# Attention and gated FFN on one Trainium2 core: the last addition of VectorE's exponential moved to accumulating DMAs, more quads on VectorE, and the second chunk of queries in two

## The chip, the core and the metric

The kernel runs on one core of one Trainium2 chip. A core has five engines with a queue each, and each works through its queue in order: TensorE (PE; its weight loads are shown as PEld), VectorE (DVE), ScalarE (ACT), GpSimd (POOL) and SyncE (SP). SP starts all the DMAs of the kernel before. The metric is the device time in microseconds (us), as the median of several runs. A profile describes one single execution.

## The reference

One transformer block of 2048 tokens, width 640, 32 heads of 20 elements, with a gated FFN of width 1728. Arrays are bf16.

```python
x = A_x                                        # [1, 2048, 640]
h = x + _A_ref(_layernorm(x), A_wqkv, A_wo)    # softmax attention, 32 heads of 20, then @ wo
h2 = h + _B_ref(_layernorm(h), B_w_gate, B_w_up, B_w_down)   # (gelu(x Wg) * (x Wu)) Wd
return h2
```

The scores are 32 x 2048 x 2048 = 134 million numbers, and the exponential of every one of them has to be computed. That is the bulk of the element-wise work.

## The kernel before

**Tiles and quads.** Scores are computed transposed: keys lie on the 128 partitions and queries along the row. A *tile* is one PSUM bank of 512 columns of scores for one head. A *quad* is the four tiles of four heads that share a group g of the heads. There are 2048 tiles, or 512 quads. Queries are taken in *chunks* (`SIZES`: 512, 512, 256, 256, 256, 128, 128). A chunk is divided into *slots* of 16 quads (64 tiles) each; there are 32 slots, numbered 0 to 31. With 512 queries a slot is one head group, with 256 queries it is two groups, with 128 it is four.

**Two engines compute the exponential.** Most tiles go to ACT: one ACTIVATE reads two or three neighbouring PSUM banks (1024 or 1536 columns) and writes bf16 to `pts` or `pts2`. Some quads go to DVE instead; `D_QUADS` gives their number for each slot, 68 in all. DVE's way (`d_exp`, L881 and the lines after it) reads a tile from PSUM, scales it and writes int16 (this is the eviction, 512 columns at a time). When two tiles (1024 columns; slots below 18) or four tiles (2048 columns, "wide"; slots from 18 on) are together in a buffer `v`, six more operations follow: mask out the low bits to `df`; a linear function to `dw`; `dw*dw`; `dw` times the masked bits; `v += dw`; and a closing scale, whose int16 result, read as bf16, is the exponential. All six run on DVE. The buffers for `v` are taken in turn from pools named e (first chunk), l (slots 8 to 17) and w (from slot 18 on); they lie in spare parts of SBUF and in the parts of `qt_all` whose queries are done. There is one `df` and one `dw` for each pool.

**PSUM.** Eight banks. ACT's tiles alternate between two sets of banks (`PAT`): sets of three and two (five banks), or, in the slots named in `SIX` (8 to 15), three and three. Bank 6 collects the sums of probabilities and V for a slot. The banks that are left, 7 and 5 or in the six-bank slots 7 alone, hold everything else (projections, FFN, transposes). A DVE tile takes one of these, or in a six-bank slot the third bank of a set.

**Units.** A *unit* is what one ACTIVATE covers: two or three tiles, with at most one DVE tile beside it. `D_LEAD` says by how many tiles a slot's DVE tiles are computed ahead of their place (24 for later slots). `D_LAG` (9) says how many units after the last DVE tile of a quad PE's products with V for this quad are put in the program.

**What sets the order.** A planner (`Sched`) orders everything. Each operation has an engine, a planned duration, a priority, and what it reads and writes; the planner plays the program through with these durations and so fixes each engine's order. In it the engines then wait for each other by semaphores. A DMA has a planned issue time on its engine and a planned latency until it lands (`lat`). PE gets filler products (`sc.pad`, `sc.warm`) where it would be idle too long.

**The rest of a slot and a chunk.** At the end of a slot, `epilogue` copies bank 6 to `osb` (two buffers, used in turn), PE transposes it (L1039), and DVE divides by the sums of probabilities into `o_nat`, which has four places of 128 queries. When a chunk's last slot is done, `post` runs its second half as background work: DMA transposes (in the tail and for the first chunk PE's) of `o_nat`, the output projection and the residual into `h_sb` (L1087), LayerNorm with its rsqrt on POOL, the normalised rows into `xn_t`, DMA transposes of these to `hnT`, then the gate products, whose raw results wait in `ha_f` (L1155), one batch of gelu on ACT with a table load before and after it, the up products and their multiplication (L1169), the down products and the last residual (L1204), and the store to `out`. `BASE` says which of the four places of `h_sb`, `hnT` and `o_nat` a chunk begins at, so a chunk's `post` has to wait for an earlier chunk that used the same places. `MERGE` names chunks whose gelu waits for that of the next chunk; it is empty.

Of the kernel before, what the change touches and what calls it, by code (L numbers as in the profile page):

```python
# [7 lines left out]
ALU = mybir.AluOpType  # L8
AX = mybir.AxisListType
FP32 = mybir.dt.float32  # L10
# [305 lines left out]
SIZES = (512, 512, 256, 256, 256, 128, 128)  # L316
BASE = (0, 0, 0, 2, 0, 2, 3)
SIX = tuple(range(8, 16))
# [26 lines left out]
def bass_sequential_preLN__mha_block__glu_gated_geglu__prompt_kernel(  # L345
# [12 lines left out]
    with ExitStack() as es:  # L358
# [3 lines left out]
        def sb(name, shape, dt=BF16):  # L362
            return es.enter_context(nc.sbuf_tensor(name, shape, dt))
# [17 lines left out]
        sel = sb("sel", [128, NA, H])  # L381
        zer = sb("zer", [128, 32])
        sel0 = sb("sel0", [128, 4, 32])
# [46 lines left out]
        aq = [carve(512) for _ in range(2)] + [sq[:], xn_t[:, 0, 0:512], xn_t[:, 1, 0:512]]  # L430
# [26 lines left out]
        dw1 = carve(1024).bitcast(F16)  # L457
        carve = carver(qt_all[:, 0, :, :].rearrange("p g s -> p (g s)"), NG * 512)
        dvw += [carve(2048).bitcast(I16) for _ in range(2)]
        dv.append(dvx[:].bitcast(I16))  # L460
        zb = dvx[:].rearrange("p (i s) -> p i s", i=2)
        dv0 = [ha_f[:, 1024 * i:1024 * i + 1024].bitcast(I16) for i in range(5)]
        df0, dw0 = ha_f[:, 5120:6144], ha_f[:, 6144:7168].bitcast(F16)
        carve = carver(qt_all[:, 1, :, :].rearrange("p g s -> p (g s)"), NG * 512)
        df2 = carve(2048)
        dw2 = carve(2048).bitcast(F16)
# [42 lines left out]
        cst(I("memset", sel[:], -1.0), "sel", 160)  # L509
        cst(I("affine_select", out=sel[:], in_=sel[:], compare_op=ALU.is_ge, fill=0.0, base=0,  # L510
              pattern=[[128, NA], [-DH, H]], channel_multiplier=1), "sel", 160)
        cst(I("affine_select", out=sel[:], in_=sel[:], compare_op=ALU.is_ge, fill=0.0, base=DH - 1,
              pattern=[[-128, NA], [DH, H]], channel_multiplier=-1), "sel", 160)
        cst(I("memset", sel0[:], 0.0), "sel0")
# [77 lines left out]
        def ln_apply(eng, src, dst, dkey, t, rkeys, prio, first=False):  # L592
            if eng == "act":
                fn = I("activation", dst, src, ACT.Identity, bias=nm[:, t:t + 1], scale=rs[:, t:t + 1])
            else:
                fn = I("tensor_scalar", dst, src, mu[:, t:t + 1], rs[:, t:t + 1], ALU.add if first else ALU.subtract,
                       ALU.mult)
            return op(eng, fn, 0.82 if eng == "act" else c_dve(D, 0.46), prio,
                      reads=list(rkeys) + [("mu", t), ("rs", t)] + ([("nm", t)] if eng == "act" else []), writes=[dkey])
# [68 lines left out]
        def aqk(t):  # L668
            return ("xn", t - 3) if t >= 3 else ("aq", t)
# [99 lines left out]
        def q_bound0(banks, prio):  # L769
# [3 lines left out]
                bank(bk), sel0[:].rearrange("p j e -> p (j e)"), aq[0], start=True, stop=True),  # L773
# [77 lines left out]
        d_cur = [None]  # L851
        d_late = []
# [9 lines left out]
        def d_exp(b, tile, prio, u):  # L862
# [15 lines left out]
            keys = [("dv", i)] + ([("dv", ("l", k)) for k in ((0, 1), (2, 3), ())[i[1]]] if kind == "w" and i[1] < 3 else [])  # L878
            aft = tuple(e_ops) + (q_done(0) if c else ()) + (q_done(1) + tuple(d_late) if kind == "w" else ()) + \
                (q_done(2) if kind == "w" and i[1] > 2 else ())  # L880
# [12 lines left out]
            d(I("tensor_scalar", dw, zi, CA / OCT, CB, ALU.mult, ALU.add), 0.265, ["df"], ["dw"])  # L893
# [130 lines left out]
        def epilogue(s_, bk, d_sums):  # L1024
# [4 lines left out]
            op("dve", I("tensor_copy", osb[:, s, :], PS[:, 512 * 6:512 * 7]), c_dve(512), P_QK,  # L1029
               reads=[("O", s_)], writes=[("osb", s)], rel=[bk], after=tuple(d_sums))  # L1030
# [7 lines left out]
            for tt in range(4):  # L1038
                op("pe", lambda eng, tt=tt: eng.transpose(bank(b2)[:, tt * 128:(tt + 1) * 128],  # L1039
                                                          osb[:, s, tt * 128:(tt + 1) * 128], identf[:]),  # L1040
                   c_mm(128, 2.5), P_EPI, mode="full", reads=[("osb", s), "identf"], writes=[key], acq=[b2] if tt == 0 else [],
                   after=tuple(aft) if tt == 0 else ())
# [22 lines left out]
        def post(c, first_banks, banks, tail):  # L1065
# [33 lines left out]
            for tt in range(tb, tb + nt):  # L1099
                t = q0 // 128 + tt - tb  # L1100
                ln_apply("dve", h_sb[:, tt, :], xn_t[:, t % 2, :], ("xn", t % 2), t, [("h", tt, 0), ("h", tt, 1)], pd)
                if tail:
                    transposes(xn_t[:, t % 2, :], [("xn", t % 2)], hnT[:, :, tt * 128:(tt + 1) * 128], ("hnT", tt),
                               first_banks, p, "act", after=first)
                else:
                    dma_transposes(xn_t[:, t % 2, :], [("xn", t % 2)], hnT[:, :, tt * 128:(tt + 1) * 128], ("hnT", tt),
# [189 lines left out]
```

## Time and profile before

| | |
|---|---|
| median of 3 runs | 914.34 us (914.05 to 917.4) |
| the profiled execution | 916.19 us |
| its span, first to last instruction | 914.2 us |
| granted TensorE clock, mean | 0.998 |
| ACT busy | 881.1 us (96% of the span) |
| PE busy | 824.1 us (90%) |
| DVE busy | 794.1 us (87%) |
| POOL busy | 48.2 us (5%) |
| DMA queue of SP | 32.89 MB, 12.9% of 16 engines' time |

The profile gives one line to each group of equal instructions: line, engine, operation, what is written and read, count, then busy time and mean length of one. Many operations are recorded by one helper (line 366), so such groups are told apart by their tiles and shapes. A PSUM bank is called `ps`. Tables of stages give, for each stretch of time, the busy time and number of instructions of each engine. Consecutive instructions on one engine overlap at their edges, so a mean length is longer than the time for which one holds the engine. PE's ends are modelled, so a busy PE is not PE at its peak.

### The profile page before, as it was taken

The numbers are of one execution on the slowest core, as the hardware profiler recorded it, in microseconds if no ns is written. First come the engines' busy times: TensorE is split into PE (matmuls) and PEld (weight loads), VectorE is DVE, ScalarE is ACT, GpSimd is POOL, SyncE is SP. The second block draws the span as 40 slices with busy tenths as digits, with TensorE's granted clock in tenths as the row PEclk, the third lists the DMA queues.
The fourth block names the chain that finished last, engine by engine and source line by source line (L and its number), as shares of the span: only waits on it lengthen the run. The fifth ranks groups of instructions, "written<-read, shape, count | busy, mean of one in ns | idle before, by whom it ended". The sixth has DMA issues, their size and how long they took to land.

```text
span 914.2 us, 22759 instructions
## 1 busy us (share of the span) xinstructions
PE 824.1 (90%) x9952; PEld 351.2 (38%) x10017; DVE 794.1 (87%) x1458; ACT 881.1 (96%) x789; POOL 48.2 (5%) x149
## 2 busy tenths in 40 slices
PE   3999999999898878899798989999999989998998
PEld 1432322222232222233233333344454445556666
DVE  8869998999899986987899997999998998779753
ACT  7999999999999999999999999999999999999982
POOL 5000000000011000000021000002010000010000
PEclk9999999999999999999999999999999999999999
DMA  7211020323801000000122000000100000110000
GB/s 259 83 31 33 23 62 25 90 67 76 291 25 30 1 1 1 1 8 16 37 35 27 1 1 1 16 30 10 37 16 18 29 1 3 36 27 10 10 17 15
DMA packets 39514, 34.33 MB, mean 38 GB/s; under 512 B 19436, under 2 KB 36936, under 8 KB 39416
## 3 DMA queue, kind: packets, MB, share of 16 engines
q1 hardware_dynamic: 39416, 32.89, 12.9%
q8 instruction: 78, 1.28, 0.6%
q14 instruction: 20, 0.16, 0.1%
HBM read 20.12 MB, written 8.09 MB: 31 GB/s over the span
## 4 chain that ended last, share of the span: by engine, by line
ACT 57%; PE 23%; DVE 17%; POOL 1%; issue 1%; DMA 0%; DVEq 0%
ACT pts L366 36%; ACT rege L366 19%; PE ps L947 6%; DVE qt_all L366 5%; PE ps L366 4%; PE ps L1120 4%; PE ps L663 4%; PE ps L1200 3%; DVE rege L366 3%; DVE qt_all L881 2%; DVE rege L881 2%; DVE rege L1169 1%; DVE rege L1155 1%; ACT L366 1%; DVE regw L701 1%
## 5 line engine op out<-in xcount | busy, mean ns | idle before, releaser
L366 ACT ACTIVATE pts<-ps 128x1024 bf16<-128x1024 f32 (+1 forms) x470 | 561.6, 1349 | 3.6 <-PE ps L947 1.5
L947 PE MATMUL ps<-qt_all,kt_all 32*128 32x256 bf16 (+2 forms) x3584 | 309.2, 289 | 44.8 <-ACT pts L366 22.0
L366 ACT ACTIVATE rege<-ps 128x1024 bf16<-128x1024 f32 (+1 forms) x233 | 288.9, 1342 | 1.9 <-PE ps L366 1.3
L947 PEld LDWEIGHTS ps<-qt_all,kt_all 32*128 32x128 bf16 x3584 | 101.4, 92 | 265.1 <-ACT pts L366 135.6
L366 DVE TENSOR_TENSOR qt_all<-qt_all 128x2048 f16<-128x2048 f16 (+3 forms) x186 | 175.0, 941 | 2.6
L1120 PE MATMUL ps<-rege,regw 128*128 128x256 bf16 (+2 forms) x952 | 151.0, 288 | 12.1 <-ACT rege L366 3.5
L366 PE MATMUL ps<-pts,v_all 128*21 128x256 bf16 (+2 forms) x2070 | 125.4, 291 | 0.4 <-DVE osb L366 0.4
L881 DVE TENSOR_SCALAR qt_all<-ps 128x512 int16<-128x512 f32 x128 | 87.4, 683 | 20.0 <-PE ps L947 19.5
L1120 PEld LDWEIGHTS ps<-rege,regw 128*128 128x128 bf16 x980 | 72.5, 98 | 71.2 <-issue 30.5
L881 DVE TENSOR_SCALAR rege<-ps 128x512 int16<-128x512 f32 x128 | 87.5, 684 | 11.0 <-PE ps L947 10.3
L366 PE MATMUL ps<-rege,v_all 128*21 128x256 bf16 (+2 forms) x1214 | 91.9, 294 | 2.6 <-DVE rege L366 2.3
L663 PE MATMUL ps<-regw 128*128 128x320 bf16 (+1 forms) x340 | 82.5, 353 | 4.2 <-ACT regw L611 1.7
L366 DVE TENSOR_SCALAR qt_all<-qt_all 128x1024 f16<-128x1024 int16 (+2 forms) x153 | 84.0, 557 | 1.9
L1200 PE MATMUL ps<-regw,rege 128*128 128x320 bf16 x448 | 80.6, 302 | 2.0 <-DVE rege L1169 1.0
L366 DVE TENSOR_TENSOR rege<-rege 128x1024 f16<-128x1024 f16 (+1 forms) x90 | 61.4, 683 | 0.8
L366 PEld LDWEIGHTS ps<-pts,v_all 128*21 128x21 bf16 x2070 | 45.1, 91 | 34.8 <-issue 29.3
L1169 DVE TENSOR_TENSOR rege<-rege,ps 128x512 bf16<-128x512 bf16 (+1 forms) x53 | 35.6, 677 | 21.9 <-PE ps L1120 21.8
L1200 PEld LDWEIGHTS ps<-regw,rege 128*128 128x128 bf16 x448 | 36.3, 97 | 34.4 <-issue 16.0
L366 DVE TENSOR_SCALAR rege<-rege 128x1024 int16<-128x1024 int16 (+2 forms) x115 | 48.3, 436 | 0.5
L366 PE MATMUL ps<-kt_all,zer 128*32 128x512 bf16 x560 | 46.9, 384 | 0.0
L663 PEld LDWEIGHTS ps<-regw 128*128 128x128 bf16 x360 | 28.4, 99 | 45.0 <-issue 24.5
L366 PEld LDWEIGHTS ps<-rege,v_all 128*21 128x21 bf16 x1214 | 31.1, 91 | 22.6 <-issue 12.1
(105 smaller groups left out, 587.9 us busy)
## 6 DMA issues: line engine op xcount, KB each, us to landing
rege<-in_A_x_dram SPq DMA_DIRECT2D x6, 640.0 KB, 5.2
q_rows<-regw SPq DMA_DIRECT2D x20, 128.0 KB, 1.7
out_dram<-rege SPq DMA_DIRECT2D x16, 160.0 KB, 2.5
regw<-in_B_w_gate_dram SPq DMA_DIRECT2D x1, 2160.0 KB, 8.4
regw<-in_B_w_up_dram SPq DMA_DIRECT2D x1, 2160.0 KB, 13.4
regw<-in_B_w_down_dram SPq DMA_DIRECT2D x1, 2080.0 KB, 19.8
kt_all<-k_rows SPq DMA_DIRECT2D x12, 160.0 KB
qt_all<-q_rows SPq DMA_DIRECT2D x12, 160.0 KB
```

What stands on the lines that cost most here:

```text
L366: return lambda eng: getattr(eng, method)(*args, **kwargs)
L663: yield op("pe", lambda eng, l=l, r=r, k=k: eng.matmul(bank(bk, n), l, r, start=(k == 0), stop=(k == len(steps) - 1)), c_mm(n) + cold, pri ...
L701: e = op("dve", lambda eng: eng.tensor_copy(dst, bank(bk)), c_dve(512), prio, reads=[key], writes=[dkey], rel=[bk], after=after)
L881: d_ops.append(op("dve", lambda eng: eng.tensor_scalar(v[:, 512 * h:512 * h + 512], bank(b), EXP_MUL, -32000.0, ALU.mult, ALU.max), c_dve( ...
L947: return lambda eng: eng.matmul(out()[:, kk * nq:(kk + 1) * nq], kt_all[32 * j:32 * j + 32, g, kt * 128:(kt + 1) * 128], qt_all[32 * j:32 ...
L1120: op("pe", lambda eng, a=a, f=f, fi=fi: eng.matmul(bank(bk)[:, fi * nq:(fi + 1) * nq], w[:, a, F0[f]:F0[f] + 128], hnT[:, a, 128 * tb:128 ...
L1155: cp.append(op("dve", lambda eng, bg=bg, fv=fv, w=w: eng.tensor_copy(fv, bank(bg, w)), c_dve(w), p, reads=[kg], writes=hkeys(k), rel=[bg], ...
L1169: hdone.append(op("dve", lambda eng, bu=bu, fv=fv, w=w: eng.tensor_tensor(fv, fv, bank(bu, w), ALU.mult), c_dve(w), p, reads=[ku] + hkeys( ...
L1200: op("pe", lambda eng, f=f, o=o, hf=hf, bk=bk: eng.matmul(bank(bk, 320), ha_f[:, o:o + 128], wd[:, f, hf * 320:(hf + 1) * 320], start=(f = ...
```

## The change

- The last addition of DVE's exponential, `v += dw`, becomes a DMA that POOL issues and that accumulates from SBUF into SBUF, in slots 1, 2, 3, 5 and 9 to 31 (`DA_SLOTS`). The product before it is written as int16 for that. The planner counts 0.95 us for the issue and then 4.67 us (1024 columns) or 7.0 us (2048 columns) until the sum has landed. DVE's closing scale waits for it. Slots 0, 4, 6, 7 and 8 keep the addition on DVE. There are 90 such DMAs.
- `dw` gets two buffers for each pool, and the pools of `v` get more: six, six, and four (six once the third quarter of the queries is done).
- `D_QUADS`: slots 18 to 27 have three DVE quads each instead of three and two in turn; 73 quads in all.
- `D_LEAD` for slots from 11 on is 42 tiles instead of 24; `D_LAG` is 8 instead of 9.
- The second chunk of 512 queries becomes two chunks of 256, and `MERGE` joins the gelu, up and down steps of these two, so that they run together after slot 15. The six-bank slots are 8 to 11 alone.
- For room in SBUF: `osb` has one buffer; `xn_t` and `sq` are gone, and LayerNorm's rows are written over `o_nat`; `sel`, `sel0` and some of the buffers of the first phase lie in the new buffers `dvx` and `dwx`.

```diff
-SIZES = (512, 512, 256, 256, 256, 128, 128)
-BASE = (0, 0, 0, 2, 0, 2, 3)
-SIX = tuple(range(8, 16))
+SIZES = (512, 256, 256, 256, 256, 256, 128, 128)
+BASE = (0, 0, 2, 0, 2, 0, 2, 3)
+SIX = tuple(range(8, 12))
...
-D_LAG = 9
-MERGE = ()
+D_LAG = 8
+MERGE = (1,)
+DA_ISSUE, DA_LAT = 0.95, 7.0
+DA_SLOTS = (1, 2, 3, 5) + tuple(range(9, 32))
...
-D_QUADS = (1,) + (2,) * 15 + (2, 2) + (3, 2) * 5 + (2, 2, 2, 2)
+D_QUADS = (1,) + (2,) * 15 + (2, 2) + (3,) * 10 + (2, 2, 2, 2)
...
-D_LEAD = ((0,) * 8, (0, 10, 20) + (24,) * 21)
+D_LEAD = ((0,) * 8, (0, 10, 20) + (42,) * 21)
...
-        osb = sb("osb", [128, 2, 512], FP32)
+        osb = sb("osb", [128, 512], FP32)
...
-        sq = sb("sq", [128, 512])
-        xn_t = sb("xn_t", [128, 2, D])
-        dvx = sb("dvx", [128, 1024])
+        dvx = sb("dvx", [128, 2048])
+        dwx = sb("dwx", [128, 2048])
...
-                pool = [(kind, i) for i in range(5 if kind != "w" or CHUNKS[slots[units[u][0][0]][0]][0] >= 1536 else 3)]
+                busy |= set(("w", k) for k, ks in enumerate(((0, 1), (2, 3), (), (4, 5))) if any(("l", x) in busy for x in ks))
+                n_ = {"e": 6, "l": 6, "w": 6 if CHUNKS[slots[units[u][0][0]][0]][0] >= 1536 else 4}[kind]
+                pool = [(kind, i) for i in range(n_)]
...
+            d_alt[0] += 1
+            a_ = d_alt[0] % len(dw)
+            dk = ("dw", a_)
+            dw = dw[a_]
+            di, dw = dw.bitcast(I16), dw.bitcast(F16)
...
-            d(I("tensor_tensor", dw, dw, dw, ALU.mult), 0.53, ["dw"], ["dw"])
-            d(I("tensor_tensor", dw, dw, zi, ALU.mult), 0.53, ["df", "dw"], ["dw"])
-            d(I("tensor_tensor", v, v, dw, ALU.add), 0.53, ["dw", ("dv", i)], [("dv", i)])
+            d(I("tensor_tensor", dw, dw, dw, ALU.mult), 0.53, [dk], [dk])
+            if tile[0] in DA_SLOTS:
+                d(I("tensor_tensor", di, dw, zi, ALU.mult), 0.53, ["df", dk], [dk])
+                d_ops.append(op(POOL, I("dma_start", v, di, accum_op=ALU.add), DA_ISSUE, prio, reads=[dk], writes=[("dv", i)],
+                                sem="da%s%d" % i, lat=DA_LAT * (w_ + 1) / 3))
+            else:
+                d(I("tensor_tensor", dw, dw, zi, ALU.mult), 0.53, ["df", dk], [dk])
+                d(I("tensor_tensor", v, v, dw, ALU.add), 0.53, [dk, ("dv", i)], [("dv", i)])
...
-                ln_apply("dve", h_sb[:, tt, :], xn_t[:, t % 2, :], ("xn", t % 2), t, [("h", tt, 0), ("h", tt, 1)], pd)
+                ln_apply("dve", h_sb[:, tt, :], o_nat[:, tt, :], [("on", g, tt) for g in range(NG)], t, [("h", tt, 0), ("h", tt, 1)], pd)
```

More of the change, by code (lines that the diff above doesn't have):

```diff
@@ L429, in bass_sequential_preLN__mha_block__glu_gated_geglu__prompt_kernel @@
         qoff = carve(512)
-        aq = [carve(512) for _ in range(2)] + [sq[:], xn_t[:, 0, 0:512], xn_t[:, 1, 0:512]]
+        aq = [carve(512) for _ in range(2)] + [dvx[:, 1024:1536], dvx[:, 1536:2048], dwx[:, 0:512]]
         carve = carver(regw, W_WORDS)
@@ L668, in aqk @@
         def aqk(t):
-            return ("xn", t - 3) if t >= 3 else ("aq", t)
+            return ("aq", t)
         STEP = {1: (1, 3), 2: (3, 4), 3: (4, 6), 4: (6, 8)}
@@ L772, in q_bound0 @@
             w_readers.append(op("pe", lambda eng: eng.matmul(
-                bank(bk), sel0[:].rearrange("p j e -> p (j e)"), aq[0], start=True, stop=True),
+                bank(bk), sel0.rearrange("p j e -> p (j e)"), aq[0], start=True, stop=True),
                 c_mm(512), prio, mode="full", util=0.213, reads=[("aq", 0), "sel0"], writes=[key], acq=[bk]))
@@ L851, in bass_sequential_preLN__mha_block__glu_gated_geglu__prompt_kernel @@
         d_cur = [None]
+        d_alt = [0]
         d_late = []
@@ L1028, in epilogue @@
             nt = nq // 128
-            op("dve", I("tensor_copy", osb[:, s, :], PS[:, 512 * 6:512 * 7]), c_dve(512), P_QK,
-               reads=[("O", s_)], writes=[("osb", s)], rel=[bk], after=tuple(d_sums))
+            op("dve", I("tensor_copy", osb[:], PS[:, 512 * 6:512 * 7]), c_dve(512), P_QK,
+               reads=[("O", s_)], writes=["osb"], rel=[bk], after=tuple(d_sums))
             b2 = Bank(*BGC[c])
```

42 lines of the change are left out of this document (23 added, 19 removed).

## The prediction

> **What bounds the kernel now.** I read four views: the page's first and fourth parts, a table of busy time by stage, the groups by shape, and the timeline of single stretches. First, the whole:
>
> ```profile
> PE 824.1 (90%) x9952; PEld 351.2 (38%) x10017; DVE 794.1 (87%) x1458; ACT 881.1 (96%) x789; POOL 48.2 (5%) x149
> ...
> ACT 57%; PE 23%; DVE 17%; POOL 1%; issue 1%; DMA 0%; DVEq 0%
> ...
> q1 hardware_dynamic: 39416, 32.89, 12.9%
> ```
>
> ScalarE (ACT) is the busiest engine and holds most of the chain that ended last; DMA is nearly idle. Now by stage, with cuts at the ends of slots 7, 11, 15, 17 and 27 and at the last exponential (columns: length, then busy us and count of PE, PEld, DVE, ACT, POOL, then clock, DMA share, GB/s):
>
> ```profile
> 33.30:242.60 209.30, 194.68 (x1560) 60.01 (x1580) 186.52 (x374) 207.03 (x182) 0.62 (x1) 1.00 0.23 67
> 242.60:352.40 109.80, 94.02 (x802) 28.32 (x811) 98.55 (x197) 109.74 (x93) 8.04 (x28) 1.00 0.14 43
> 352.40:453.90 101.50, 89.01 (x772) 28.94 (x779) 86.39 (x164) 101.50 (x88) 0.00 (x0) 1.00 0.05 14
> 453.90:506.10 52.20, 46.19 (x640) 19.02 (x647) 48.43 (x98) 52.05 (x47) 8.43 (x28) 1.00 0.18 27
> 506.10:773.20 267.10, 252.14 (x3337) 116.02 (x3349) 250.78 (x379) 265.84 (x231) 10.91 (x28) 1.00 0.06 14
> 773.20:881.60 108.40, 101.42 (x2333) 65.07 (x2336) 82.28 (x137) 106.49 (x92) 7.28 (x28) 0.98 0.10 20
> 881.60:914.20 32.60, 27.99 (x381) 22.98 (x379) 13.18 (x32) 11.02 (x14) 0.00 (x0) 1.00 0.05 16
> ```
>
> From 33.3 to 881.6 us ACT is busy 843 of 848 us, so what the change is worth there is ACT time taken away, as long as VectorE (DVE) keeps up. DVE's room differs: 11% idle in slots 0-7, 10 to 15% in slots 8-15, but 6% in slots 18-27 (250.78 of 267.10). There, slot by slot:
>
> ```profile
> 506.10:531.60 25.50, 23.86 (x303) 9.62 (x306) 25.27 (x38) 25.30 (x24) 0.00 (x0) 1.00 0.01 1
> ...
> 564.50:590.20 25.70, 23.63 (x325) 9.67 (x327) 25.51 (x38) 25.70 (x24) 0.00 (x0) 1.00 0.07 15
> 590.20:612.70 22.50, 22.10 (x301) 9.84 (x300) 20.52 (x31) 22.41 (x21) 0.00 (x0) 1.00 0.10 31
> ```
>
> Slots with three DVE quads (18, 20) leave DVE under 0.3 us; one with two (21) leaves 2 us. All five added quads go into slots of this stage, so DVE is the second bound.
>
> **The change, part by part.**
>
> *Five more quads on DVE (68 to 73).* A quad is four tiles of 512 columns, so ACT loses 20 tiles. Its shapes:
>
> ```profile
> L366 ACT ACTIVATE pts<-ps 128x1536 bf16<-128x1536 f32 x249 | 377.3, 1550 | 3.4 <-PE ps L947 1.5 <-PE ps L366 0.9
> L366 ACT ACTIVATE pts<-ps 128x1024 bf16<-128x1024 f32 x221 | 243.9, 1122 | 0.2
> L366 ACT ACTIVATE rege<-ps 128x1536 bf16<-128x1536 f32 x121 | 185.4, 1551 | 1.9 <-PE ps L366 1.3 <-PE ps L947 0.4
> L366 ACT ACTIVATE rege<-ps 128x1024 bf16<-128x1024 f32 x112 | 124.2, 1116 | 0.0
> ...
> 328.27 3.11 ACT L366 ACTIVATE pts<-ps 128x1536 bf16<-128x1536 f32 x2
> 330.95 3.12 ACT L366 ACTIVATE rege<-ps 128x1536 bf16<-128x1536 f32 x2
> ```
>
> A tile is 1550 - 1122 = 428 ns. The last two rows start 2.68 us apart, so instructions overlap and a three-tile one holds the engine for 1.34 us: 1.34 - 3 x 0.428 = 0.056 us is fixed. 20 tiles: -8.56 us. Walking the loop that forms units with the old constants gives 370 and 333 instructions of three and two tiles, as the rows have (249+121, 221+112); with the new ones 356 and 344 (1756 tiles, which is (512-73) x 4). Three fewer: -0.17 us. That already includes four more in slots 12-15, where the six-bank pattern becomes three and two banks. ACT: -8.7 us.
>
> *The final addition of DVE's exp goes to an accumulating DMA on POOL*, except in slots 0, 4, 6, 7 and 8. What DVE pays:
>
> ```profile
> L366 DVE TENSOR_TENSOR rege<-rege 128x1024 int16<-128x1024 int16 x30 | 20.5, 682 | 0.2
> ...
> L366 DVE TENSOR_TENSOR qt_all<-qt_all 128x2048 f16<-128x2048 f16 x51 | 61.9, 1214 | 0.6
> L881 DVE TENSOR_SCALAR qt_all<-ps 128x512 int16<-128x512 f32 x69 | 47.0, 683 | 5.3 <-PE ps L947 5.1
> L366 DVE TENSOR_SCALAR qt_all<-qt_all 128x2048 int16<-128x2048 int16 x36 | 24.1, 677 | 0.2
> L366 DVE TENSOR_TENSOR qt_all<-qt_all 128x2048 int16<-128x2048 int16 x18 | 21.8, 1209 | 0.1
> L1155 DVE CAST rege<-ps 128x512 bf16<-128x512 f32 x24 | 16.3, 680 | 0.0
> ```
>
> A wide quad (slots 18 on) is 4 evictions of 0.68, 3 multiply-or-mask operations of 0.68 and 3 two-input operations of 1.21: 8.4 us; without the last addition 7.2. In slots 18-27: 25 additions go (-30 us), 5 quads come (+36 us): +6 us, on a stage that ACT wants 8.7 us shorter (258.4). DVE would stand at 256.8 of it. Elsewhere it gains: 8 early quads and 18 in slots 9-17 lose two additions of 0.68 each (-35 us), slots 28-31 lose 8 of 1.21 (-10 us); all beside ACT, so worth nothing by itself.
>
> *The second chunk of queries in two, its two FFNs joined.* Table loads stay: six batches of gelu before and after, over the same columns. But the first half's output projection, LayerNorm and gate products can start after slot 11 instead of slot 15. They wait for the first chunk's last outputs, since they reuse its rows of h_sb:
>
> ```profile
> 402.95 22.61 SPq L366 DMA_DIRECT2D out_dram<-rege  x3
> 437.06 0.39 SPq L366 DMA_DIRECT2D rege<-in_A_x_dram  x1
> 437.50 0.51 SPq L366 DMA_DIRECT2D out_dram<-rege  x1
> 457.04 6.02 SPq L366 DMA_TRANSPOSE rege<-o_nat  x4
> ...
> 437.50:453.90 16.40, 12.10 (x128) 3.60 (x130) 13.81 (x27) 16.40 (x16) 0.00 (x0) 1.00 0.17 51
> ```
>
> So they fall into about 415-455 us, where DVE and PE have room, and 7 gate evictions and the like (7 x 0.68 + 4 x 0.48 and LayerNorm: about 8 us of DVE) leave the time after slot 15. I count 6 of them off the tight stage: DVE 251 of 258.4 us, 97%. 256-wide products instead of 512-wide double PE's weight loads for these queries; the row of slots 16-17, 256 wide already, has ACT at 52.05 of 52.20, so I cost it at nothing; PE's idle time of 12% in slots 12-15 is the cover, and without it the extra loads (512 of scores at 92 ns by the next row, four at a time) would be some 12 us.
>
> ```profile
> L947 PEld LDWEIGHTS ps<-qt_all,kt_all 32*128 32x128 bf16 x3584 | 101.4, 92 | 265.1 <-ACT pts L366 135.6 <-ACT rege L366 70.0 <-issue 31.6
> ```
>
> *The DMA itself.* DVE runs in order, and its closing scale waits for the landing; evictions of scores are queued behind it, PE's next scores wait for those banks, and ACT for PE. The order gives issue and landing 0.95 + 4.67 = 5.6 us for 1024 columns (256 KB), 0.95 + 7.0 = 7.95 us for 2048 (512 KB). No accumulating DMA is in the trace. Nearest rows (KB each, us to landing):
>
> ```profile
> rege<-in_A_x_dram SPq DMA_DIRECT2D x6, 640.0 KB, 5.2
> q_rows<-regw SPq DMA_DIRECT2D x20, 128.0 KB, 1.7
> rege<-in_A_x_dram SPq DMA_DIRECT2D x3, 320.0 KB, 3.1
> rege<-o_nat SPq DMA_TRANSPOSE x11, 2.7
> ```
>
> 320 to 640 KB costs 2.1 us: about 1.0 us + 6.6 ns per KB. As plain copies the two sizes are 2.7 and 4.4 us (lower end). Counting the bytes twice, because the destination is read too, gives 4.4 and 7.7; four times (upper end) 7.7 and 14.4. I take twice, between ends far apart, since an addition must at least fetch both operands: just in time, so no wait, and up to 6.7 us of DMA time for each of the 38 wide sums. That is new company for the transposes of the FFN (2.7 us):
>
> ```profile
> L663 PE MATMUL ps<-wo,rege 128*128 128x320 bf16 x160 | 28.8, 302 | 1.5 <-DMA rege<-o_nat 0.6 <-DVE rege L1087 0.3 <-issue 0.3
> ```
>
> PE now waits 0.6 us for them in all; if each of the 26 were delayed by its own length with nothing else to do, 70 us; I take nothing, because PE has scores and sums of other tiles in between. Behind an issue that waits on POOL for DVE's product stand only LayerNorm's small steps, and behind these the FFN, which is background. On SP nothing is added.
>
> *The rest.* LayerNorm written over o_nat makes slot 8's epilogue wait for the transposes that in this trace run at 274-282 us (slot 8 ended at 269.9); only the one osb buffer hangs on it, until slot 9 ends 26 us later: nothing. Removed buffers cost no time. D_LEAD 42 starts quads 18 tiles, some 8 us, earlier to pay for the DMA.
>
> **Sum.** Span 914.2 - 8.7 = 905.5; +1 us for DVE at 97%, as the tight slots above lose 0 to 0.2 us of ACT each and about five join them: 906.5. The profiled execution took 916.19 us, 2.0 outside its span; the median of the runs, 914.34, is 1.85 below it and 0.14 above the span. On the median: 914.34 - 7.7 = **906.6 us**.
>
> **The rivals.**
>
> (a) *The sum lands late and DVE stands still: slower.* Place: the closing scale of slots 18-27, 30 waits. Price: 30 x L against about 7 us of DVE room in that stage, and the 8.7 us gained. At L = 0.55 us (30 x 0.55 = 16.5) the gain is gone; L = 1 us gives 914.3 - 8.7 + 23 = 929 us; the four-times bound (L = 6.5) over 1000. What speaks for it: POOL is hindered beside DVE in this trace:
>
> ```profile
> 633.78 1.07 POOL L366 CAST mv<-mv 128x4 bf16<-128x4 f32 x1 [150.52 <-DVE mv L366]
> 634.93 1.20 POOL L366 TENSOR_SCALAR sd<-mv 128x2 bf16<-128x2 bf16 x1
> 636.08 0.18 POOL L366 CAST mu<-mv 128x2 f32<-128x2 bf16 x1
> ...
> 633.63 2.43 DVE L366 TENSOR_TENSOR qt_all<-qt_all 128x2048 f16<-128x2048 f16 x2
> ```
>
> Work on four elements or fewer takes 0.18 us in the third row and 1.07 to 1.20 in the first two, which lie beside DVE's two-input operations (fourth row); an issue that loses such a 1 us is late by L = 0.75 after my reserve of 0.25 us: 914.3 - 8.7 + (22.5 - 7) = 921 us. Against: with the bytes counted once the reserve is 3.5 us and swallows it. The Trainium skill (SBUF — State Buffer, Who interferes with whom) speaks for this case: it says that DVE and GpSimd share one pair of ports, that DVE's two-port modes lock GpSimd out for a whole instruction, and that descriptors which GpSimd writes for a DMA are held up by it. The trace agrees that POOL stretches; that it holds for an issue no run here shows. The other half of (a) is a sum that itself takes longer, at 929 us and above.
>
> (b) *DVE becomes the bound in slots 18-27.* If the FFN work doesn't leave the stage (256.8 of 258.4) and waits on PE of some 6 us (the 5.1 in the eviction row) stay, the stage is 263: the gain shrinks to about 4 us, 910 to 914 us.
>
> (c) *The additions are hidden anyway and relief of DVE also shortens ACT's small stalls.* Between 33.3 and 881.6 ACT shows 5 us idle: at best 902.
>
> **How the numbers follow.** Forecast (903 to 909.7) 0.46; (a) 0.34, half by a hindered issue (921) and half by a slow sum (929 and more), of which 0.04 lies within 0.5%; (b) 0.16, 0.12 of it within 0.5% and 0.04 faster, when less of the PE wait stays; (c) 0.04. A measurement of this kernel tells about 0.5%, 4.6 us, from no change. Faster 0.46 + 0.04 + 0.04 = 0.54, less 0.04 because the forecast lies only 3 us from that bound: 0.50; same 0.04 + 0.12 + 0.04 = 0.20; slower 0.30. The range runs from 902 (c) to (a) at L = 1, 929; above it stays 0.15, for a much slower sum.
>
> **What would show it.** Right: 356 and 344 activations; POOL with 90 DMA issues; DVE's closing operations waiting for DMA under 5 us in all; ACT still busy above 98% until the last exponential, some 8 us earlier. Wrong: a group of DVE waits on DMA of tens of us, or the same time as DVE idle behind PE, ACT idle in slots 18-27, transposes slower than 2.7 us. If the landings need over 8.5 us for 512 KB, (a) decides.

## The result and the profile after

The changed kernel takes 913.70 us in the median of 20 runs (912.5 to 915.76); the kernel before, on the same chip, 914.59 us (913.88 to 917.4). The ratio is 0.9985, with a 95% interval from 0.9979 to 0.9991. The gain is 0.9 us, 0.1%, where 7.7 us were predicted; by the prediction's bound of 0.5% that is the same time.

First rows of the changed kernel's page and of its list of DMAs: span, busy time of the engines, shares of the chain that ended last, and DMA issues (KB each, median us to landing).

```profile
span 913.0 us, 25152 instructions
...
PE 832.7 (91%) x11135; PEld 383.4 (42%) x11180; DVE 763.3 (84%) x1426; ACT 871.2 (95%) x786; POOL 134.2 (15%) x239
...
ACT 68%; PE 19%; DVE 7%; DMA 2%; POOL 2%; issue 1%; SPq 0%
...
qt_all<-dwx POOLq DMA_DIRECT2D x11, 512.0 KB, 5.8
qt_all<-qt_all POOLq DMA_DIRECT2D x11, 512.0 KB, 5.1
...
rege<-rege POOLq DMA_DIRECT2D x16, 256.0 KB, 3.6
...
rege<-o_nat SPq DMA_TRANSPOSE x26, 3.3
```

ACT has 9.9 us less work than before (881.1) and DVE 30.8 us less (794.1). Yet the span is only 1.2 us shorter. The table of stages, with the same cuts as before (first exponential, ends of slots 7, 11, 15, 17 and 27, last exponential, end), shows where the rest is; the columns are length, busy us and count of PE, PEld, DVE, ACT, POOL, then clock, DMA share and GB/s.

```profile
32.90:244.60 211.70, 197.53 (x1553) 60.15 (x1570) 180.97 (x359) 206.69 (x183) 15.09 (x17) 1.00 0.40 104
244.60:347.20 102.60, 88.05 (x1292) 34.40 (x1305) 93.16 (x194) 100.89 (x88) 20.88 (x42) 1.00 0.26 44
347.20:458.10 110.90, 100.71 (x1287) 42.85 (x1295) 84.05 (x168) 110.84 (x98) 17.71 (x31) 1.00 0.31 57
458.10:509.60 51.50, 47.03 (x688) 22.61 (x688) 42.33 (x82) 51.50 (x47) 10.20 (x21) 1.00 0.30 55
509.60:764.20 254.60, 240.94 (x3363) 114.55 (x3360) 240.84 (x375) 251.08 (x219) 40.09 (x58) 0.98 0.39 76
764.20:876.30 112.10, 108.04 (x2430) 71.81 (x2430) 79.22 (x135) 111.63 (x97) 17.37 (x35) 1.00 0.28 50
876.30:913.00 36.70, 32.29 (x399) 26.35 (x397) 14.86 (x35) 11.01 (x14) 0.00 (x0) 1.00 0.05 19
```

| stage | before, us | after, us | difference |
|---|---|---|---|
| start to first exponential | 33.3 | 32.9 | -0.4 |
| slots 0-7 | 209.3 | 211.7 | +2.4 |
| slots 8-15 | 211.3 | 213.5 | +2.2 |
| slots 16-17 | 52.2 | 51.5 | -0.7 |
| slots 18-31 | 375.5 | 366.7 | -8.8 |
| after the last exponential | 32.6 | 36.7 | +4.1 |
| span | 914.2 | 913.0 | -1.2 |

Slots 18-27 and 28-31 are taken together, since one batch of gelu moved across their border, as another did across slot 11's. The predicted 8.7 us are there, though the match to a tenth is luck: TensorE's granted clock stood at a half for 3.4 us of slots 28-31 in the profiled run before and for 10.2 us of slots 18-27 in the one after. The kernel without early sums, below, has the same quads in these slots, was profiled without a half clock, and takes 363.6 us for them. The gain is given back in three places: before slot 8, between slots 8 and 15, and after the last exponential. What stands after the last exponential is seen in the timeline of the changed kernel (start, length, engine, operation, and in brackets the wait before it).

```profile
874.58 3.29 PE L1138 MATMUL ps<-rege,regw 128*128 128x256 bf16 x32
...
876.28 1.28 ACT L368 ACT_TABLE_LOAD   x1
...
878.43 2.06 PE L1218 MATMUL ps<-regw,rege 128*128 128x320 bf16 x14
...
886.58 3.29 PE L1218 MATMUL ps<-regw,rege 128*128 128x320 bf16 x23
...
889.90 0.49 DVE L1222 TENSOR_TENSOR rege<-ps,rege 128x320 bf16<-128x320 f32 x1 [0.75 <-PE ps L1218]
```

The down products (L1218) of the sixth chunk run behind the table load that follows the last exponential, until 889.9 us. In the kernel before, the down products of its last 256-wide chunk were over as that point came: its table load is at 881.61, its last residual at 881.80.

```profile
881.61 1.28 ACT L366 ACT_TABLE_LOAD   x1
881.80 0.49 DVE L1204 TENSOR_TENSOR rege<-ps,rege 128x320 bf16<-128x320 f32 x1 [2.77 <-PE ps L1200]
```

### The profile page after: what moved, and what is told of

Its sections match the earlier page's. It is cut to its first block, busy times and chain, and to the rows that moved or that the text cites. A ratio compares the mean times of both kernels' runs of the same rounds, so it can differ in the third digit from the quotient of the medians.

```text
span 913.0 us, 25152 instructions
## 1 busy us (share of the span) xinstructions
PE 832.7 (91%) x11135; PEld 383.4 (42%) x11180; DVE 763.3 (84%) x1426; ACT 871.2 (95%) x786; POOL 134.2 (15%) x239
## 4 chain that ended last, share of the span: by engine, by line
ACT 68%; PE 19%; DVE 7%; DMA 2%; POOL 2%; issue 1%; SPq 0%
ACT pts L368 43%; ACT rege L368 24%; PE ps L965 5%; PE ps L667 4%; PE ps L1138 3%; PE ps L368 3%; PE ps L1218 3%; DMA regw<-in_A_wqkv_dram 1%; ACT L368 1%; DVE qt_all L368 1%; DVE rege L889 1%; DVE qt_all L889 1%; DVE dwx L368 1%; POOL nw L368 1%; DVE rege L368 1%
## 5 line engine op out<-in xcount | busy, mean ns | idle before, releaser
L368 ACT ACTIVATE pts<-ps 128x1536 bf16<-128x1536 f32 (+1 forms) x468 | 556.1, 1352 | 5.1 <-PE ps L965 2.7
L368 ACT ACTIVATE rege<-ps 128x1536 bf16<-128x1536 f32 (+1 forms) x232 | 289.7, 1359 | 5.5 <-PE ps L368 3.8
L965 PEld LDWEIGHTS ps<-qt_all,kt_all 32*128 32x128 bf16 x4096 | 108.6, 92 | 252.6 <-ACT pts L368 130.5
L1138 PEld LDWEIGHTS ps<-rege,regw 128*128 128x128 bf16 x1120 | 85.9, 98 | 61.4 <-issue 27.0
L889 DVE TENSOR_SCALAR qt_all<-ps 128x512 int16<-128x512 f32 x116 | 79.5, 686 | 12.0 <-PE ps L965 11.1
L667 PE MATMUL ps<-regw 128*128 128x512 bf16 (+1 forms) x345 | 84.2, 351 | 4.7 <-DMA regw<-in_A_wqkv_dram 1.6
L1218 PE MATMUL ps<-regw,rege 128*128 128x320 bf16 x448 | 78.1, 301 | 1.7 <-DVE rege L1222 0.8
L368 DVE TENSOR_TENSOR qt_all<-qt_all 128x2048 int16<-128x2048 f16 (+3 forms) x79 | 74.2, 940 | 1.0
L368 PEld LDWEIGHTS ps<-pts,v_all 128*21 128x21 bf16 x2338 | 53.9, 91 | 32.3 <-issue 26.9
L368 DVE TENSOR_SCALAR qt_all<-qt_all 128x2048 int16<-128x2048 int16 (+3 forms) x111 | 63.5, 574 | 1.0
L368 DVE TENSOR_TENSOR rege<-rege 128x1024 f16<-128x1024 f16 (+1 forms) x74 | 50.6, 684 | 0.9
L1218 PEld LDWEIGHTS ps<-regw,rege 128*128 128x128 bf16 x448 | 37.4, 97 | 30.5 <-issue 13.6
```

Of the source, the lines that this page charges most:

```text
L368: return lambda eng: getattr(eng, method)(*args, **kwargs)
L667: yield op("pe", lambda eng, l=l, r=r, k=k: eng.matmul(bank(bk, n), l, r, start=(k == 0), stop=(k == len(steps) - 1)), c_mm(n) + cold, pri ...
L889: d_ops.append(op("dve", lambda eng: eng.tensor_scalar(v[:, 512 * h:512 * h + 512], bank(b), EXP_MUL, -32000.0, ALU.mult, ALU.max), c_dve( ...
L965: return lambda eng: eng.matmul(out()[:, kk * nq:(kk + 1) * nq], kt_all[32 * j:32 * j + 32, g, kt * 128:(kt + 1) * 128], qt_all[32 * j:32 ...
L1138: op("pe", lambda eng, a=a, f=f, fi=fi: eng.matmul(bank(bk)[:, fi * nq:(fi + 1) * nq], w[:, a, F0[f]:F0[f] + 128], hnT[:, a, 128 * tb:128 ...
L1218: op("pe", lambda eng, f=f, o=o, hf=hf, bk=bk: eng.matmul(bank(bk, 320), ha_f[:, o:o + 128], wd[:, f, hf * 320:(hf + 1) * 320], start=(f = ...
```

## The experiments

Theory S, formed on these tables: the exponentials got shorter as predicted, but the FFN's background work on PE doesn't fit beside them any longer and comes out behind the last exponential; the early sums and the split cost some us each. Rival Q says that the quads pay in full and something else lost the time, W puts the loss into late sums, and others say that the order merely fell out otherwise. All diffs are against the changed kernel unless another is named; the medians of before are of the same chip.

### The quads alone undone

```diff
-D_QUADS = (1,) + (2,) * 15 + (2, 2) + (3,) * 10 + (2, 2, 2, 2)
+D_QUADS = (1,) + (2,) * 15 + (2, 2) + (3, 2) * 5 + (2, 2, 2, 2)
```

> The changed kernel with 68 quads again (slots 18 to 27 with three and two in turn). Theory S (spill): the FFN is background work that needs its own time beside the exponentials; what the five quads took from ACT came out in slots 18 to 31, but the FFN then ended after the last exponential. Without them the last exponential ends about 8.5 us later than in the changed kernel (876.3 to 885), the time after it falls from 36.7 to about 31 us, and the total stays within 3 us of 913.7. Rival Q (the quads pay in full, and something else lost it): the time after the last exponential stays at 36 to 37 us and the total is about 922 us.

Measured: 917.09 us (914.13 to 919.61, 10 runs), 1.002 times the kernel before (1.0005 to 1.0036; before 914.54). Its last stages:

```profile
509.30:776.60 267.30, 251.18 (x3451) 123.60 (x3449) 221.54 (x346) 265.98 (x231) 31.65 (x53) 0.99 0.32 63
776.60:885.00 108.40, 101.63 (x2345) 65.76 (x2346) 73.03 (x127) 105.65 (x92) 14.29 (x35) 0.97 0.28 56
885.00:914.40 29.40, 24.12 (x326) 19.99 (x327) 11.19 (x28) 9.63 (x13) 0.00 (x0) 1.00 0.04 13
```

The last exponential ends at 885.0 and the tail is 29.4 us. So the five quads take 267.3 + 108.4 - 366.7 = 9.0 us from the exponentials, and the tail takes 36.7 - 29.4 = 7.3 us of that back. S holds on the tail and Q falls. With 29 us of DVE's work gone from slots 18-27 (250.78 before, 221.54 here) nothing became faster. The median is 3.4 us above the changed kernel's, just outside S's 3 us; at the same granted clock of 0.998 the spans are 912.1 to 913.5 us here and 910.7 to 912.0 there, so the five quads are worth some 1 to 2 us in all, 9.0 less 7.3.

The FFN is behind long before the last exponential. By its table load, the first gelu batch of slots 18-31 starts at much the same time in both kernels (522.3 us here, 524.0 in the changed kernel); the next three start at 650.6, 742.2 and 837.2 us here, and at 704.7, 791.2 and 861.2 there. So the added quads hold the FFN back within slots 18-27. What it lacks there isn't settled: PE shows 22.9 us idle in slots 18-31 here and 17.7 us in the changed kernel, more than the 56 down products in its tail need (23 of them took 3.29 us), and a DVE tile also takes one of the PSUM banks that the FFN uses. No run separates PE's time from the banks or from the planned order.

### Less FFN after the last exponential

The kernel of the next experiment, with the down products of the sixth chunk taken over 4 of their 14 blocks (so its output isn't the reference's):

```diff
-                    for f in range(NF):
+                    FS = range(4) if c == 5 else range(NF)
+                    for f in FS:
```

> Early additions on DVE as in the second run of this study, and the down products of the sixth chunk (the last of 256 queries) over 4 of its 14 blocks of the hidden width only (it leaves out 40 products of PE, 40 x 0.136 = 5.4 us, so this chunk's output is not the reference's). Theory S: this FFN is what stands after the last exponential, so the time after it falls from 36.7 to 32 or 33 us, the last exponential stays at 872 us, and the total falls by 3 to 5 us, to 906 to 908. Rival: the time after the last exponential is set by the last chunk's own chain (output projection, LayerNorm, FFN), PE had room beside it, and it stays at 36 to 37 us.

Measured: 907.90 us (907.4 to 912.4, 4 runs), ratio 0.9924 (0.9903 to 0.9946), where the same kernel with all its FFN has 911.21 and 0.9955. The last stage:

```profile
877.50:910.30 32.80, 27.20 (x359) 22.47 (x357) 14.66 (x35) 11.00 (x14) 0.00 (x0) 0.99 0.06 21
```

40 products of 320 columns less shorten the tail by 3.9 us (36.7 to 32.8), and the time falls by 0.3%, about 3 us. They do stand on the path. (Expected were 32 or 33 us of tail and 906 to 908 us in all.)

### The early sums back on DVE

```diff
-DA_SLOTS = (1, 2, 3, 5) + tuple(range(9, 32))
+DA_SLOTS = tuple(range(9, 32))
```

> The changed kernel with the additions of slots 1, 2, 3 and 5 back on DVE. Theory E: these 16 early sums made slots 0 to 7 longer (209.3 us before, 211.7 after), since their quads have no lead and the closing scale comes late in the slot; without them the stretch is back at about 209.3 us, and the total is 911 to 912 us, or unchanged if the time after the last exponential grows by as much. Rival: the 2.4 us come from the SBUF and buffer moves or from chance, and the stretch stays at 211 to 212 us.

Measured: 911.21 us (909.95 to 913.25, 6 runs), ratio 0.9955 (0.994 to 0.9969). Its first and last stages:

```profile
32.90:242.30 209.40, 194.79 (x1569) 60.08 (x1587) 186.64 (x375) 207.08 (x183) 0.62 (x1) 1.00 0.23 68
...
871.90:908.60 36.70, 32.28 (x399) 26.33 (x397) 14.85 (x35) 11.00 (x14) 0.00 (x0) 1.00 0.06 19
```

Slots 0-7 are back at 209.4 us (209.3 before) and the tail hasn't moved, so the sums of the eight early quads (two each) cost 2.3 us there. Slots 8-15 give 0.9 of it back: they take 214.4 us here and 213.5 in the changed kernel. The medians differ by 2.5 us (913.70 to 911.21), but five of these six runs have a clock of 1.000 and only two of the changed kernel's 20; at 1.000 the spans are 908.2 to 909.4 us here, with a median of 909.1, and 910.4 and 910.6 there. So early sums cost about 1.4 us net, and the rest of the difference goes with the clock. The changed kernel's waits of ACT in slots 0-7 show how; in the kernel without early sums the first row reads 1.1 us in one wait.

```profile
ACT rege L368 <- PE ps L368: 3.8, 2, 2.8
ACT pts L368 <- PE ps L368: 0.9, 2, 0.5
```

ACT stands still for 2.8 us at one place (92.6 to 95.3 us, the end of slot 1), where its buffer of probabilities waits for PE's products with V, and those stand in PE's queue behind the end of the slot and the projections of later groups. A sum that takes 3.6 us to land (the median of these 16), where DVE's addition takes 0.68, moves the products of its quad back in that queue. This last link is read from the timeline; no run isolates it.

### No sums at all

```diff
-DA_SLOTS = (1, 2, 3, 5) + tuple(range(9, 32))
+DA_SLOTS = ()
```

> The changed kernel with every last addition on DVE again, 73 quads, second chunk in two: DVE does 85 us more. Theory: DVE is the second bound; with the additions it cannot keep up in slots 18 to 27, ACT stands still there, and the total is 922 to 930 us, so the sums do pay for the five quads. Rival: DVE's relief was hidden beside ACT, and the total stays at 911 to 914 us.

Measured: 929.55 us (927.37 to 933.5, 4 runs), ratio 1.0155 (1.0129 to 1.0181; before 915.03). Slots 18-27:

```profile
507.50:788.00 280.50, 262.16 (x3611) 124.27 (x3615) 272.01 (x407) 256.10 (x223) 10.19 (x28) 0.98 0.05 13
```

With 73 quads and every addition on DVE, DVE is busy for 272 of 280 us and ACT waits 24 us. The sums therefore do what they are for: against 929.55 they are worth 16 us. They take 67 us off DVE (830.3 us busy here, 763.3 in the changed kernel), where 85 were expected. Without them DVE, the second bound of the prediction, has no room for the five quads.

### The second chunk whole again

```diff
-SIZES = (512, 256, 256, 256, 256, 256, 128, 128)
+SIZES = (512, 512, 256, 256, 256, 128, 128)
```

with `BASE`, `SIX` and `MERGE` of before.

> The changed kernel with the second chunk of 512 queries in one piece again, six banks in slots 8 to 15, no merged FFN. Theory S: its projection and gate products, some 8 us of DVE and as much of PE, fall after slot 15 again, and the time after the last exponential grows from 36.7 to 45 us or so; slots 8 to 15 are back at 211 us from 213.5; total 918 to 924 us. Rival: the split only cost the 2.2 us in slots 8 to 15, and without it the total is about 911.5 us.

Measured: 923.05 us (922.55 to 927.0, 4 runs), ratio 1.0095 (1.0064 to 1.0126). The last stage, and slots 8-11 and 12-15:

```profile
245.10:346.90 101.80, 88.45 (x775) 26.25 (x785) 92.10 (x189) 100.76 (x89) 20.39 (x42) 1.00 0.24 44
346.90:457.60 110.70, 95.09 (x796) 30.57 (x804) 79.99 (x152) 110.64 (x94) 14.85 (x17) 1.00 0.26 51
...
873.40:921.20 47.80, 43.57 (x531) 36.66 (x528) 21.38 (x45) 14.21 (x17) 0.00 (x0) 1.00 0.04 15
```

Without the split the tail is 47.8 us, 11 more: the second chunk's gelu starts at 576.3 us instead of 524.0, and the later batches at 747.0 and 819.0 instead of 704.7 and 791.2. Slots 8-15 take 212.5 us here, where 211 were expected, 213.5 with the split and 211.3 before. So the split itself costs 1.0 us there, and 1.2 come from the rest of the change. The sums aren't the reason for these: without any sum (the run before this one) slots 8-15 take 213.6 us.

### The sums given less time in the order

```diff
-DA_ISSUE, DA_LAT = 0.95, 7.0
+DA_ISSUE, DA_LAT = 0.95, 5.0
```

> The changed kernel with 5.0 instead of 7.0 us of planned latency for a wide sum (3.3 instead of 4.7 for a narrow one); the order alone changes. In the trace of after a wide sum takes 5.2 us from issue in the median and 7.7 at most, a narrow one 3.3 and 5.2; the order allowed 7.95 and 5.6, and would now allow 5.95 and 4.3. Theory A (allowed too much): chains end earlier, buffers come free earlier, the FFN gets on and less of it is left after the last exponential: 909 to 912 us, with DVE waiting for sums under 3 us. Rival W (the wait takes its place): about one wide sum in eight lands later than the order thinks, DVE stands still at the closing scale and everything behind it: 915 us or more, with over 5 us of DVE waits on DMA.

Measured: 926.85 us (924.5 to 928.82, 4 runs), ratio 1.0124 (1.01 to 1.0148). One place in its timeline, and the windows around it:

```profile
449.03 0.88 POOL L368 DMA_DIRECT2D qt_all<-dwx  x1 [1.09 <-DVE dwx L368]
449.11 5.28 SPq L368 DMA_TRANSPOSE rege<-o_nat  x2
...
456.48 0.43 DVE L368 TENSOR_SCALAR qt_all<-qt_all 128x1024 int16<-128x1024 int16 x1 [3.19 <-DMA qt_all<-dwx]
```

```profile
440.00:450.00 10.00, 9.86 (x139) 4.31 (x136) 9.22 (x21) 10.00 (x11) 7.33 (x17) 1.00 0.35 70
450.00:460.00 10.00, 6.33 (x73) 3.02 (x66) 4.44 (x9) 7.01 (x7) 0.86 (x1) 0.81 0.80 68
460.00:470.00 10.00, 10.00 (x85) 3.94 (x83) 5.06 (x9) 6.53 (x7) 0.85 (x1) 0.50 0.27 68
```

A sum of 256 KB, issued at 449.03, lands only as the wait ends at 456.48, 7.4 us later, beside two DMA transposes; the changed kernel's sums of this size take 3.3 us in the median. DVE waits 3.19 us, PE falls to 6.3 of 10 us, and in the next window the granted clock is 0.50, so PE needs all of 10 us for 85 products and ACT gets to work 6.5 us. A late sum costs more than its own wait: all waits of DVE for sums come to 7.7 us, and the span is 13.7 us longer than the changed kernel's. This is the prediction's rival (a), brought about by an order that allows too little; the changed kernel's 7.0 keeps clear of it.

### Quads moved, to fill DVE's room elsewhere

The kernel without early sums; `D_LAG` 9; no sums in slots 16, 25, 28 and 30; of the 73 quads, slot 9 has one less, slot 14 one more, slot 25 one less, and of slots 28-31 the second (29) has one more. The aim was to let the FFN catch up.

```diff
-D_LAG = 8
+D_LAG = 9
-DA_SLOTS = (1, 2, 3, 5) + tuple(range(9, 32))
+DA_SLOTS = (9, 10, 11, 12, 13, 14, 15, 17, 18, 19, 20, 21, 22, 23, 24, 26, 27, 29, 31)
-D_QUADS = (1,) + (2,) * 15 + (2, 2) + (3,) * 10 + (2, 2, 2, 2)
+D_QUADS = (1, 2, 2, 2, 2, 2, 2, 2, 2, 1, 2, 2, 2, 2, 3, 2, 2, 2, 3, 3, 3, 3, 3, 3, 3, 2, 3, 3, 2, 3, 2, 2)
```

> A version that might beat both: no early sums, 73 quads with one each moved out of slots 9 and 25 into slots 14 and 29 (slot 28 stays at two), the sums of slots 16, 25, 28 and 30 on DVE, so that the FFN is served better; the allowed times unchanged. Theory S: with the same 73 quads and the FFN less behind, the time after the last exponential is 32 to 34 us instead of 36.7 and the total 904 to 908 us. Rival: the place of the quads does not matter, 911 us as in the second run.

Measured: 911.18 us (910.27 to 911.42, 5 runs), ratio 0.995 (0.9936 to 0.9963). The tail is 33.3 us as expected, but the total was missed: slots 18-31 take 259.1 + 109.6 = 368.7 us, 5.1 more than in the kernel without early sums (363.6). The total is what the rival expected (911 us), but its stages moved: less tail, longer exponentials. The last row is the tail.

```profile
506.20:765.30 259.10, 244.02 (x3420) 118.39 (x3422) 242.78 (x378) 254.54 (x221) 34.36 (x54) 0.99 0.35 69
765.30:874.90 109.60, 105.84 (x2392) 70.12 (x2391) 85.83 (x145) 109.12 (x94) 12.10 (x33) 1.00 0.22 42
874.90:908.20 33.30, 29.75 (x375) 24.30 (x372) 13.36 (x33) 11.68 (x16) 0.00 (x0) 1.00 0.06 21
```

### Quads moved, with a little less time for the sums

```diff
-D_LAG = 8
-DA_ISSUE, DA_LAT = 0.95, 7.0
-DA_SLOTS = (1, 2, 3, 5) + tuple(range(9, 32))
-D_QUADS = (1,) + (2,) * 15 + (2, 2) + (3,) * 10 + (2, 2, 2, 2)
+D_LAG = 6
+DA_ISSUE, DA_LAT = 0.95, 6.3
+DA_SLOTS = (10, 11, 12, 15, 16, 17, 18, 19, 20, 21, 22, 23, 24, 25, 26, 27, 29, 30, 31)
+D_QUADS = (1, 2, 2, 2, 2, 2, 2, 2, 2, 2, 2, 2, 2, 2, 3, 2, 3, 0, 3, 3, 3, 3, 3, 3, 3, 3, 3, 3, 2, 2, 3, 1)
```

> Another such version with 74 quads, sums in fewer slots, and 6.3 instead of 7.0 us allowed for a wide sum (7.25 with the issue; 5.15 for a narrow one). Theory W, as the third run had it: allowances near the slow landings let single sums come late, PE falls idle and its clock is halved for some us; with 7.25 us most wide sums still land in time, so 903 to 910 us, but if single late ones are met, 912 to 920 us with a granted clock under 0.99. Rival: the third run's loss came from the shorter order itself, and this version also loses without a late sum.

(These are 73 quads, not 74.) Measured: 911.68 us (907.6 to 915.08, 10 runs), ratio 0.9958 (0.9937 to 0.9979). The tail is 29.7 us, but around 461 us DVE waits 1.7 us for a sum beside transposes, and what follows is the picture of the run with less time:

```profile
460.00:466.00 6.00, 3.49 (x49) 1.99 (x47) 3.79 (x8) 5.24 (x5) 0.74 (x1) 0.98 1.10 182
466.00:476.00 10.00, 9.63 (x80) 3.36 (x81) 4.41 (x10) 5.14 (x5) 1.71 (x2) 0.50 0.31 55
```

Five of the ten runs have a mean clock of 0.987 and spans of 911.8 to 913.0 us; the other five have 0.992 or more and 905.5 to 907.4. So both outcomes that W named occur, in different runs of one program; the median lies between them.

### The same, with DMA transposes reckoned at their true time

```diff
-... sem=f"xp{wkey[1]}", lat=2.0, after=after)
+... sem=f"xp{wkey[1]}", lat=3.4, after=after)
```

> The kernel of the run with quads moved and less time (e8), with one number changed: the order now reckons 3.4 us instead of 2.0 for a DMA transpose, which is what they took in the changed kernel (3.3 us). Theory W (e8 lost its gain where a sum landed late beside transposes, and to the half clock of TensorE behind that): with the transposes given their true time the wait of 1.7 us at 461 us goes, the half clock at 466 to 476 us with it, slots 16-17 fall from 59.6 to 52-54 us, the tail stays 30-32, and the time is 905 to 909 us. Rival L (what e8 lost there is only another order of the work and comes back in another stage): slots 16-17 fall, but the sum of the stages does not, 910 to 914 us.

Measured: 909.98 us (906.23 to 913.07, 7 runs), ratio 0.9936 (0.9915 to 0.9957; before 915.13). Slots 16-17 and the tail:

```profile
452.50:507.40 54.90, 53.63 (x718) 26.72 (x712) 38.36 (x73) 53.69 (x48) 7.59 (x20) 0.97 0.27 52
...
877.70:908.10 30.40, 26.36 (x355) 21.67 (x352) 12.54 (x31) 6.78 (x12) 0.00 (x0) 1.00 0.07 23
```

Slots 16-17 fall from 59.6 to 54.9 us, and DVE's wait for the sum there falls from 1.7 to 1.1 us; it doesn't go away. W expected 52 to 54 us there and 905 to 909 in all, so both lie 1 us outside, and 909.98 us is as near to rival L's lower end of 910. The experiment doesn't decide between them: at a clock of 0.996 the spans are 906.1 and 907.9 us here and 905.5 to 906.7 in the run before, so what is gained is that no run falls to 0.987. The single runs order themselves by the clock again: 904.1 us of span at 1.000, 905.7 at 0.998, 911.0 at 0.991. It has the lowest median of all kernels that compute everything; its interval and that of the kernel without early sums overlap.

### More filler on PE

The kernel without early sums, with:

```diff
-PAD_WIN, PAD_MIN = 3.4, 0.42
+PAD_WIN, PAD_MIN = 3.4, 0.5
```

> The kernel without early sums (e2), with one number changed: TensorE is given filler products until 0.50 instead of 0.42 of each 3.4 us is work. Theory K (the granted clock falls to a half for some microseconds in most runs since TensorE idles a little too long, and each such window costs 1 to 2 us): more of the runs stand at a mean clock of 0.999 to 1.0 and the median falls by about 1 us from e2's 911.2, to 909.5 to 910.5, with the spread of the runs within 1.5 us. Rival P (the filler stands in the way of scores, or the windows of half clock come from waits that no filler covers): same clock, 911 us or more.

Measured: 917.48 us (916.07 to 920.58, 10 runs), ratio 1.0023 (1.001 to 1.0035). The clock isn't better (0.994 to 0.998; with the filler as it was five of six runs had 1.000), as rival P has it. Theory K falls as far as filler goes. But the order changed with it, and the waits of DVE show sums that came late (the same row has 0.8 us in the kernel without early sums), so what the filler costs by itself stays open.

```profile
DVE qt_all L368 <- DMA qt_all<-qt_all: 6.0, 3, 3.7
```

## Why the prediction was wrong, by its own steps

- **"ACT: -8.7 us"** was right. The two groups of exponentials count 356 and 344 instructions, as worked out, and slots 18-31 are 8.8 us shorter. Quads alone (first experiment): 9.0.
- **The DMA itself** was right in its verdict. Counting the bytes twice gave "4.4 and 7.7" us; measured 3.2 to 5.2 us for 256 KB (median 3.3) and 4.5 to 7.7 for 512 KB (median 5.2). So the estimate was above the median by 1.1 and 2.5 us; the longest wide sum meets it, the longest narrow one passes it by 0.8. Rival (a) didn't come: all waits of DVE for sums are in one row of the changed kernel. The transposes did get slower (3.3 us in the median instead of 2.7), which the prediction names as a sign of being wrong; but PE waits for them 1.0 us in all (0.6 before), so the nothing that was taken for it was about right.

```profile
DVE rege L368 <- DMA rege<-qt_all: 1.0, 1, 1.0
```

- **POOL hindered in issuing** was seen, and did no harm. Per group the row gives shortest, median and longest ns of one issue:

```profile
L368 POOL DMA_DIRECT2D qt_all<-dwx x17: 858/895/1389, 296.5 to 844.3; - x17
```

  An issue takes 1.39 us at worst, where 0.95 was planned. That is in line with the Trainium skill (SBUF — State Buffer, Who interferes with whom), which says that DVE's two-port modes hold GpSimd up, though which of DVE's operations stood beside the long issues isn't sorted out here. The 0.5 us over the shortest issue fall into the 1.8 us by which the median landing of a wide sum is under its planned 7.0.
- **DVE at 97%** came to 95%, 240.84 of 254.60 us where 251 of 258.4 were worked out. The size of a quad was off: the mean lengths added up to 7.2 us for a wide quad without its last addition, and the five quads add 29.3 us to DVE (763.3 against 734.0 with 68 quads), 5.9 us each. Rival (b) isn't what happened, though 913.70 us lies in its range of 910 to 914: it needed 263 us in slots 18-27, and they took 254.6.
- **The step that failed** is the one that took what stands after the last exponential as given: "Span 914.2 - 8.7 = 905.5", with the FFN only as work "which is background". The FFN had its place beside ACT's exponentials, and with the stretch shorter the down products of the sixth chunk came out behind it. I looked at ACT and DVE as bounds and never at what the FFN would still have to do at the last exponential: +4.1 us, of which the quads alone make 7.3 and the rest of the change -3.2. PE is busy 240.94 of 254.60 us in slots 18-27 and 108.04 of 112.10 in slots 28-31, so little place was left on it; that PE, and not the banks or the planned order, held the FFN back is argued.
- **"all beside ACT, so worth nothing by itself"**, of the early sums: they cost 2.3 us in slots 0-7, about 1.4 net. The step allowed no loss, though the prediction itself counts some us from a DMA's issue to its landing, where DVE's addition takes 0.68.
- **The split, "so I cost it at nothing"**: it costs 1.0 us in slots 8-15 and saves 11 us of tail. The saving was missed, since the step looked at DVE's room in the tight stage and not at the tail. There it was near: DVE is busy 245.69 us in slots 18-27 without the split and 240.84 with it, 4.9 us less where 6 were counted. 1.2 us in slots 8-15 aren't assigned by any run.
- **The standing of the profiled run, "1.85 below it"**: the kernel before has most of its runs at a clock of 1.000 with spans of 912.0 to 913.3 us; the profiled one had 0.998 and 914.2. To apply the -7.7 to the median took for granted that the changed kernel would have as many runs at 1.000; it has 2 of 20 (spans 910.4 and 910.6), 11 at 0.998 (median 911.5) and 7 below. About 1 us of the gain goes here.

In sum: -8.8 and -0.7 and -0.4 us gained, 2.4 + 2.2 + 4.1 given back, -1.2 us of span, and 0.9 in the medians.

## What to carry to other kernels

When the engine that bounds a kernel is given less work, look for what was running beside it: add up what that work still has to do at the moment when the bound ends, and count it as the new tail. An operation that moves from an engine to a DMA brings a latency that shows where the order is tight, even on an engine with time to spare, so move only those that the busy stage needs. What the order assumes for a DMA should be its time beside the other DMAs that run with it.

## What was not expected of the hardware

- DMA transposes are slowed by accumulating sums: in the changed kernel the 18 that ran beside one took 4.4 us from issue to landing in the median, the 8 others 2.6; in the kernel with no sums at all the median of the 26 is 2.7. The sums themselves mostly aren't slowed: beside a transpose 3.3 us in the median for 256 KB and 5.2 for 512, as without one. But single ones are, up to 7.4 us for 256 KB in the kernel with less time. Whether the DMA engines or the memory set that isn't shown.
- The half clock. In the changed kernel's profile three windows of 5 us show it (length, then the columns of the stage table; the clock is the third number from the right):

```profile
565.00:570.00 5.00, 4.11 (x50) 1.54 (x44) 4.29 (x9) 4.30 (x4) 1.17 (x1) 0.70 0.28 56
...
590.00:595.00 5.00, 4.09 (x41) 1.48 (x42) 4.45 (x8) 4.03 (x4) 0.00 (x0) 0.59 0.00 0
595.00:600.00 5.00, 4.75 (x56) 2.47 (x57) 3.26 (x8) 3.99 (x4) 3.55 (x8) 0.73 0.21 40
```

  ACT, which should be full, is busy 4.0 to 4.3 of 5 us there. The Trainium skill (TensorE: Matmul & The Clock Gate, What's actually happening) says that the clock falls to a half after a free-running window of about 3.4 us in which PE had too little work. The traces agree in the size and the length: the clock is 0.50, and such stretches last 3.41 us or a multiple of it (3.41 and 6.83 in the changed kernel's profile, 17.07 in the one with less time). With less time they stand beside a stretch with PE busy 6.3 of 10 us; in the changed kernel PE shows 5.00 of 5.00 us busy just before (560 to 565 us), so the cause there isn't seen. The run-to-run spread follows it: in the kernel with the transposes' true time 904.1 us of span at a mean clock of 1.000 and 911.0 at 0.991. The 10.2 us at half clock cost the changed kernel's profiled run about 3 us: slots 18-27 take 254.6 us with them and 251.5 in the kernel without early sums, whose profile has none. That a stall of PE starts such a stretch, and that it prolongs the stall, is read from the windows; no run took the clock alone away.
